# One run of weight loads behind layer 0's transposes, and 1/den of group 0 spread by PE

## The chip, the cores and the metric

The kernel runs on one core of a Trainium2 chip. The metric is the device time of one execution in microseconds (us). Every kernel was run several times beside the kernel before on the same chip; the medians and 95% intervals below come from those runs. Times inside an execution are counted from the first instruction of the profiled run of that kernel.

## The reference

Four layers over 2048 tokens of width 512, two of linear attention and two of a gated feed-forward block, in turn and with the same weights.

```python
def _A_ref(x, wqkv, wo):                         # 32 heads of 16
    q, k, v = ...                                # x @ wqkv, split into heads
    phi = lambda t: jnp.where(t > 0, t + 1, jnp.exp(t)) + 1e-6
    pq, pk = phi(q), phi(k)
    kv = jnp.einsum("bhsd,bhse->bhde", pk, v)
    z = jnp.einsum("bhsd->bhd", pk)
    num = jnp.einsum("bhqd,bhde->bhqe", pq, kv)
    den = jnp.einsum("bhqd,bhd->bhq", pq, z)[..., None] + 1e-6
    return merge_heads(num / den) @ wo
def _B_ref(x, w_gate, w_up, w_down):             # inner width 1792
    return (silu(x @ w_gate) * (x @ w_up)) @ w_down
x = A_x
for _ in range(2):
    x = x + _A_ref(_layernorm(x), A_wqkv, A_wo)
    x = x + _B_ref(_layernorm(x), B_w_gate, B_w_up, B_w_down)
```

## The kernel before

All five engines run hand-made orders. PE follows a list of tokens: `0k3` is layer 0, k of tile 3; `0q20` is q of group 2 (four tiles of 128 tokens), part 0; `0z` sums k over the tokens, `0d` makes den, `0r2` spreads 1/den of group 2 by PE, `0m` multiplies the k-v products by Wo, `0w` is the output matmul of the layer, `1u` gate and up, `1n` down, `S` a warming filler. The other engines have lists of the operations that belong to these tokens (`0x` is a layer norm, `xT` and `rT` are DMA transposes, `pqn` is the multiplication of q by 1/den). Each engine works strictly through its own list, so an operation that waits holds up all that stand behind it.

The weights but Wq, Wk and Wv are loaded by POOL, which has four DMA lanes; a DMA on a lane waits for the one before it on that lane.

```python
pr = Prog({"sp": 8, "act": 3, "pool": 4})        # DMA lanes of each issuing engine
...
weights = []
dma("sp", Wqkv[:, :, 0:D], wq3[:, :, 0:D], w=["Wq"])
dma("sp", Wqkv[:, :, 2 * D:], wq3[:, :, 2 * D:], w=["Wv"])
weights.append(lambda a: dma("pool", Wo[:], ..., w=["Wo"], after=a))
for c in range(NC):
    weights.append(lambda a, c=c: dma("pool", Wg[:, c, :], ...))
    weights.append(lambda a, c=c: dma("pool", Wu[:, c, :], ...))
def load_down(after): ...                        # Wd in four loads on POOL
...
last = list(xT_of.values())                      # layer 0's DMA transposes
for w_ in weights:
    w_(last)                                     # i.ld .. i.ld8 on POOL
```

Three steps on POOL make a mask of blocks of 16 by 16. Zm, the sum of k laid out for the den matmuls, needs that mask, and so every den matmul of layer 0 does.

```python
def z_fin(L, pb):
    op("dve", ..., r=[f"pb{pb}", "mask"], w=["Zm"], kind="zm")     # Zm = z * mask
```

POOL's order has the last mask step, `i.c7`, behind its nine loads: `... 0x14.negm i.ld i.ld1 ... i.ld8 i.c7 1x3.negm ...`.

A value of 1/den stands for 16 columns of q. There are two ways to spread it. Groups named in `PE_T` (group 2 here) go by PE: one DVE transpose, 16 matmuls with a selecting matrix into four PSUM banks, and four DVE multiplications from PSUM. The others go by DMA: for each tile ACT makes a repeated copy (`rrep`, a ring of three buffers), a DMA transposes it into RT, and DVE multiplies.

```python
for tl in range(TG):                             # by DMA
    q = r_rrep.take()
    op("act", ..., w=[f"rrep{q}"], kind="rep")
    op("sp", lambda e: e.dma_start(RT[R][:, :, ...], rrep[q][:], transpose=True), ..., kind="rT")
    scale(L, g, tl, RT[R][...], f"RT{R}_{tl}")   # kind "pqn" on DVE
def rep_pe(L, g):                                # by PE
    bs = [bank(pin=True) for _ in range(4)]
    for c in range(NC):
        for a, pb in enumerate(bs):
            mm(pb, esel[...], rT[d][...], n=P, ...)
    ...                                          # four multiplications on DVE read the banks
```

## Time and profile before

| | before |
|---|---|
| median of the first three runs (lowest to highest) | 430.45 us (429.04 to 430.57) |
| span of the profiled run | 428.1 us |
| first den, first Wo, first gate matmul of layer 1 | 42.56, 56.60, 68.80 us |
| first gate matmul of layer 3 | 276.48 us |

A fourth run, of 429.31 us, is counted in the result below and makes the median 429.88; the profiled run took 429.86. Two rows are added here that are needed later. The first, from the page, is the PE clock that was granted in 40 slices of the span, in tenths: full speed throughout. The second is from the view of the tile RT: how long the DMA transposes of 1/den take from issue to landing.

```profile
PEclk9999999999999999999999999999999999999999
```

```profile
DMA to landing us min/median/max: 2.4/2.4/4.5
```

### The profile page before, as it was taken

Reading aid. Unit: us, or ns where it says so; the run is one execution under the profiler, and the core shown is the slowest. Engines: PE = TensorE matmul, PEld = TensorE weight load, DVE = VectorE, ACT = ScalarE, POOL = GpSimd, SP = SyncE. Lnnn points to the kernel's source line nnn. Section 1 sums busy time; section 2 is a strip of 40 time slices with the busy share of each in tenths; the row PEclk is TensorE's granted clock in tenths of the full one; section 3 lists DMA queues with packets and bytes.
Section 4 is the critical chain, followed back from the end, with each engine's and each line's share of the span. In section 5 each row is a group of like instructions: output and inputs, shape, how many; then the busy total and the mean of one; then the engine's idle time right before and its main releaser. Section 6 shows DMA issues by size and latency. Waiting matters only on the chain.

```text
span 428.1 us, 6340 instructions
## 1 busy us (share of the span) xinstructions
PE 419.4 (98%) x2219; PEld 195.5 (46%) x2219; DVE 287.8 (67%) x629; ACT 202.9 (47%) x399; POOL 83.0 (19%) x205
## 2 busy tenths in 40 slices
PE   8999899999999999999999999999999999999997
PEld 6444444444444444444444444344444444444443
DVE  6865799793675476875447869888837606853662
ACT  5998785563356264254465648445312302402220
POOL 5634035210120150001334500431002000100000
PEclk9999999999999999999999999999999999999999
DMA  8639534522011021000021113322110010021001
GB/s 277 141 75 329 126 64 101 146 50 51 4 22 37 2 52 34 2 0 2 2 48 26 25 26 63 62 46 41 38 38 0 13 51 25 0 63 37 2 0 50
DMA packets 53279, 23.21 MB, mean 54 GB/s; under 512 B 46528, under 2 KB 52160, under 8 KB 53248
## 3 DMA queue, kind: packets, MB, share of 16 engines
q1 hardware_dynamic: 51408, 16.27, 17.6%
q0 software_dynamic: 1296, 6.03, 4.1%
q10 hardware_dynamic: 544, 0.52, 0.4%
q8 instruction: 17, 0.28, 0.3%
q14 instruction: 14, 0.11, 0.1%
HBM read 9.70 MB, written 2.10 MB: 28 GB/s over the span
## 4 chain that ended last, share of the span: by engine, by line
PE 88%; DMA 5%; ACT 3%; DVE 2%; issue 1%; SPq 0%; POOL 0%; ACTq 0%; DVEq 0%
PE pb L409 88%; DMA RT<-rrep 2%; DMA xnT<-xnA 1%; DMA X<-in_A_x_dram 1%; ACT pq L567 1%; ACT etmp L564 1%; ACT rrep L719 0%; DVE pq L573 0%; ACT GT L657 0%; DVE pq L732 0%; SPq L723 0%; ACT xnA L498 0%; SPq L440 0%; DVE xnA L522 0%; ACT xnA L495 0%
## 5 line engine op out<-in xcount | busy, mean ns | idle before, releaser
L782 ACT ACTIVATE tht<-pb 128x512 f32<-128x512 f32 x112 | 65.4, 595 | 129.4 <-PE pb L409 106.8
L409 PE MATMUL pb<-xnT,Wg 128*128 128x512 bf16 x448 | 115.0, 379 | 0.6 <-issue 0.6
L409 PE MATMUL pb<-xnT,Wu 128*128 128x512 bf16 x448 | 115.0, 379 | 0.0
L784 DVE SCALAR_TENSOR_TENSOR tht<-tht,pb 128x512 f32<-128x512 f32 x112 | 75.4, 684 | 55.6 <-ACT tht L782 48.9
L409 PE MATMUL pb<-Wd,hT 128*128 128x512 bf16 (+2 forms) x462 | 99.8, 373 | 0.0
L787 DVE TENSOR_TENSOR hT<-tht,pb 128x512 bf16<-128x512 f32 x112 | 74.2, 682 | 2.8
L409 PEld LDWEIGHTS pb<-Wd,hT 128*128 128x128 bf16 x462 | 44.7, 98 | 52.3 <-DVE hT L787 0.2
L409 PEld LDWEIGHTS pb<-xnT,Wu 128*128 128x128 bf16 x448 | 43.6, 98 | 53.1 <-DVE hT L787 0.8
L409 PEld LDWEIGHTS pb<-xnT,Wg 128*128 128x128 bf16 x448 | 43.5, 98 | 53.3 <-issue 1.3
L511 POOL TENSOR_TENSOR rstd<-vpe,negh 128x1 f32<-128x1 f32 x64 | 37.4, 587 | 90.4 <-DVE vpe L507 88.3
L564 ACT ACTIVATE etmp<-pb 128x512 bf16<-128x512 f32 x64 | 37.2, 594 | 21.8 <-PE pb L409 13.1
L501 POOL TENSOR_SCALAR mv<-sums 128x1 f32<-128x1 f32 x55 | 12.8, 239 | 119.8 <-DVE X L810 62.1
L409 PE MATMUL pb<-Wqkv,xnT 128*128 128x512 bf16 x128 | 31.2, 379 | 1.2 <-DMA xnT<-xnA 0.6
L409 PE MATMUL pb<-xnT,Wqkv 128*128 128x512 bf16 x128 | 32.1, 379 | 0.0
L409 PE MATMUL pb<-pk,xnA 128*128 128x512 bf16 x128 | 31.2, 379 | 0.0
L409 PE MATMUL pb<-GT,pq 128*128 128x512 bf16 x128 | 30.2, 379 | 0.2
L498 ACT ACTIVATE xnB<-X,sums 128x512 bf16<-128x512 bf16 x32 | 22.9, 717 | 15.7 <-DVE X L762 8.8
L569 DVE TENSOR_SCALAR etmp<-etmp 128x512 bf16<-128x512 bf16 x64 | 18.7, 304 | 12.1 <-ACT etmp L564 12.0
L762 DVE SCALAR_TENSOR_TENSOR X<-pb,X 128x512 bf16<-128x512 f32 x32 | 21.6, 686 | 7.1 <-PE pb L409 7.0
L810 DVE SCALAR_TENSOR_TENSOR X<-pb,X 128x512 bf16<-128x512 f32 x16 | 11.0, 689 | 19.1 <-PE pb L409 19.0
L498 ACT ACTIVATE xnA<-X,sums 128x512 bf16<-128x512 bf16 x23 | 16.5, 717 | 12.1 <-DVE X L810 11.9
L810 DVE SCALAR_TENSOR_TENSOR pq<-pb,X 128x512 bf16<-128x512 f32 (+2 forms) x17 | 10.9, 656 | 14.4 <-PE pb L409 14.3
(77 smaller groups left out, 309.9 us busy)
## 6 DMA issues: line engine op xcount, KB each, us to landing
out_dram<-pq SPq DMA_DIRECT2D x15, 128.0 KB, 1.8
Wg<-in_B_w_gate_dram POOLq DMA_DIRECT2D x4, 448.0 KB, 4.9
Wu<-in_B_w_up_dram POOLq DMA_DIRECT2D x4, 448.0 KB, 4.6
X<-in_A_x_dram SPq DMA_DIRECT2D x6, 256.0 KB, 4.8
Wd<-in_B_w_down_dram POOLq DMA_DIRECT2D x3, 512.0 KB, 4.7
Wqkv<-in_A_wqkv_dram SPq DMA_DIRECT2D x2, 512.0 KB, 7.0
Wqkv<-in_A_wqkv_dram ACTq DMA_DIRECT2D x2, 256.0 KB, 3.5
X<-in_A_x_dram SPq DMA_DIRECT2D x4, 128.0 KB, 3.4
```

The lines of the kernel that those rows point to most:

```text
L409: return op("pe", lambda e: e.matmul(o_ap, lhsT=lhsT, rhs=rhs, start=start, stop=stop, skip_group_check=skip), r=r, w=w, n=n)
L498: op("act", lambda a: a.activation(out=b_ap, in_=X[:, t, :], func=ACT.Square, scale=-float(D), bias=sums[:, t:t + 1], accum_out=mv[:, t, 1 ...
L501: op("pool", lambda p: p.tensor_scalar(out=mv[:, t, 0:1], in0=sums[:, t:t + 1], scalar1=-1.0 / D, scalar2=None, op0=ALU.mult), r=[f"sm{t}" ...
L511: op("pool", lambda p: p.tensor_tensor(out=rstd[:, t:t + 1], in0=vpe[:, t:t + 1], in1=negh[:], op=ALU.pow), r=[f"vp{t}", "negh"], w=[f"rs{ ...
L564: op("act", lambda a: a.activation(out=etmp[e][:], in_=PB[pb][:], func=ACT.Exp), r=[f"pb{pb}"], w=[f"e{e}"], kind="exp")
L567: op("act", lambda a: a.activation(out=dst, in_=PB[pb][:], func=ACT.Identity, bias=onep[:]), r=[f"pb{pb}", "onep"], w=dk, kind="id1")
L569: op("dve", lambda v: v.tensor_scalar(out=etmp[e][:], in0=etmp[e][:], scalar1=1.0, scalar2=1e-6, op0=ALU.min, op1=ALU.add), r=[f"e{e}"], w ...
L762: op("dve", lambda v: v.scalar_tensor_tensor(out=X[:, t, :], in0=PB[pb][:], scalar=1.0, in1=X[:, t, :], op0=ALU.mult, op1=ALU.add, accum_o ...
L782: op("act", lambda e: e.activation(out=tht[a][:], in_=PB[pg][:], func=ACT.Tanh, scale=0.5), r=[f"pb{pg}"], w=[f"th{a}"], kind="tanh")
L784: op("dve", lambda v: v.scalar_tensor_tensor(out=tht[a][:], in0=tht[a][:], scalar=1.0, in1=PB[pg][:], op0=ALU.add, op1=ALU.mult), r=[f"pb{ ...
L787: op("dve", lambda v: v.tensor_tensor(out=hT[h][:, j, :], in0=tht[a][:], in1=PB[pu][:], op=ALU.mult), r=[f"pb{pu}", f"th{a}"], w=[f"h{h}_{ ...
L810: op("dve", lambda v, pb=pb, lo=lo, hi=hi: v.scalar_tensor_tensor(out=o_ap[:, lo:hi], in0=PB[pb][:, 0:hi - lo], scalar=0.5, in1=X[:, t, lo ...
```

## The change

The intent, as far as the diff shows it, is to keep the weights away from the transposes: all that POOL loads, with Wv added, goes out in one run after layer 0's transposes and ahead of layer 1's, and group 0 of layer 0 needs no DMA transposes any more because PE spreads its 1/den. The core of the diff:

```diff
-dma("sp", Wqkv[:, :, 2 * D:], wq3[:, :, 2 * D:], w=["Wv"])
+weights.append(lambda a: dma("pool", Wqkv[:, :, 2 * D:], wq3[:, :, 2 * D:], w=["Wv"], after=a))
 ...
 for w_ in weights:
     w_(last)
+load_down(last)                        # was behind layer 1's first transposes
 ...
-    PE_T = 0d2 0t0 0t1 0t2 0t3 2d1 2z
+    PE_T = 0t0 0t1 0t2 0t3 2d1 0d0 0t14 0d2
-dsb, rtok, rT: 2 buffers;  rrep: 3
+dsb, rtok, rT: 3 buffers;  rrep: 2
 ... POOL's order:
-0x14.negm i.ld i.ld1 ... i.ld8 i.c7 1x3.negm ... Wd.ld3 ... Wd.ld1 Wd.ld2 ... Wd.ld ...
+0x13.pow i.ld i.ld1 ... i.ld9 Wd.ld Wd.ld1 Wd.ld2 Wd.ld3 i.c7 1x3.negm ...
 ... PE's order:
-0q31 0m0 0m1 0m2 0m3 0r2 0w3 ...
+0q31 0m0 0r0 0m1 0m2 0r2 0m3 0w3 ...
```

Two smaller things come with it: the transposes of tile 14 go by PE, and tile 12's k is summed on DVE instead of by PE (`0z12` becomes `0s`). The orders of ACT, DVE, POOL and SP are new throughout; among other things DVE takes over copies of PE's transposes from ACT.

## The prediction

> **What bounds the kernel now.** I read the page first (busy shares, chain), then PE's timeline for its idle time, then the timelines of POOL, DVE and ACT around each idle place.
>
> ```profile
> PE 419.4 (98%) x2219; PEld 195.5 (46%) x2219; DVE 287.8 (67%) x629; ACT 202.9 (47%) x399; POOL 83.0 (19%) x205
> ...
> PE 88%; DMA 5%; ACT 3%; DVE 2%; issue 1%; SPq 0%; POOL 0%; ACTq 0%; DVEq 0%
> ```
>
> PE works for 98% of 428.1 us and carries 88% of the chain of waits. The 98% alone would prove little, so I checked it by start times: in PE's timeline four 512-column matmuls start every 0.86 us.
>
> ```profile
> 1.24 4.44 PE L409 MATMUL pb<-hT 128*128 128x128 bf16 x42 [1.24 <-DVE hT L415]
> 7.07 1.02 PE L409 MATMUL pb<-Wqkv,xnT 128*128 128x512 bf16 x4 [0.51 <-DVE xnT L553]
> 15.69 1.90 PE L409 MATMUL pb<-Wqkv,xnT 128*128 128x512 bf16 x8 [0.58 <-DMA xnT<-xnA]
> ...
> 51.88 0.46 PE L409 MATMUL pb<-Zm,pq 128*128 128x8 bf16 x12 [1.33 <-DVE pq L573]
> ```
>
> These are all the PE rows of the first 230 us with idle time in front of them (42.56, quoted below, has only 0.22 us of lost start time). So what the change can win lies in two places: 0.58 us at 15.69 (PE waits for the first DMA transpose) and 1.33 us at 51.88. The other idle places (0.3 to 0.6 us each, 248 to 277 us) belong to layer 2. Every microsecond that PE is made to wait anywhere is, on the other hand, paid in full.
>
> The 1.33 us has this cause: DVE, which works in order, stands at the multiplication of q by the transposed 1/den of group 0 and waits for the DMA; the phi step that PE needs is behind it.
>
> ```profile
> 51.06 0.43 DVE L732 TENSOR_TENSOR pq<-pq,RT 128x512 bf16<-128x512 bf16 x1 [1.83 <-DMA RT<-rrep]
> 51.40 0.42 DVE L573 TENSOR_TENSOR pq<-pq,etmp 128x512 bf16<-128x512 bf16 x1
> ```
>
> Now POOL, whose 19% makes it look harmless, with the one DVE row that depends on it:
>
> ```profile
> 31.36 0.97 POOL L440 DMA_DIRECT2D Wo<-in_A_wo_dram  x1 [6.11 <-DMA xnT<-xnA]
> 32.33 0.57 POOL L440 DMA_DIRECT2D Wg<-in_B_w_gate_dram  x1
> 32.89 0.54 POOL L440 DMA_DIRECT2D Wu<-in_B_w_up_dram  x1
> 33.42 0.54 POOL L440 DMA_DIRECT2D Wg<-in_B_w_gate_dram  x1
> 36.58 0.56 POOL L440 DMA_DIRECT2D Wu<-in_B_w_up_dram  x1 [2.61 <-DMA Wo<-in_A_wo_dram]
> 37.70 0.65 POOL L440 DMA_DIRECT2D Wg<-in_B_w_gate_dram  x1 [0.56 <-DMA Wg<-in_B_w_gate_dram]
> 38.84 0.54 POOL L440 DMA_DIRECT2D Wu<-in_B_w_up_dram  x1 [0.49 <-DMA Wu<-in_B_w_up_dram]
> 39.96 0.54 POOL L440 DMA_DIRECT2D Wg<-in_B_w_gate_dram  x1 [0.59 <-DMA Wg<-in_B_w_gate_dram]
> 41.29 0.54 POOL L440 DMA_DIRECT2D Wu<-in_B_w_up_dram  x1 [0.79 <-DMA Wu<-in_B_w_up_dram]
> 41.83 0.37 POOL L430 TENSOR_SCALAR_AFFINE_SELECT mask<-mask 128x128 bf16<-128x128 bf16 x1
> ```
>
> ```profile
> 42.30 0.21 DVE L614 TENSOR_TENSOR Zm<-pb,mask 128x32 bf16<-128x32 f32 x1 [1.61 <-POOL mask L430]
> ```
>
> ```profile
> 42.56 0.56 PE L409 MATMUL pb<-Zm,pq 128*128 128x8 bf16 x16
> ```
>
> Four loads go out at once; from the fifth on POOL stands until the load four places earlier has landed (the program gives POOL four DMA lanes). Behind the ninth load stands the last step of the block mask. DVE waits 1.61 us for it to make Zm, and PE's first den matmul follows 0.26 us later. Before the change this costs PE only those 0.22 us: the queue of loads already ends exactly where PE begins to need the mask.
>
> **What the Trainium skill says.** (1) "Trainium Kernel Development and Optimization", Performance Expectations: matmul busy time is a bad measure of closeness to the roofline because matmuls are pipelined. The trace agrees: the page gives 379 ns for one matmul of 512 columns, while the starts are 0.86/4 = 0.215 us apart; hence I count starts. (2) "TensorE: Matmul & The Clock Gate", Part 1: the PE clock is halved by default and after about one idle window of 3.4 us, and takes about 3.4 us of work to return. The trace shows the cold half: the first 42 filler matmuls of 128 columns take 4.44 us, 106 ns each, the page's cold figure. No idle stretch of before is long enough to show the fall back; the change could make one. (3) "DMA: Bandwidth & Descriptors", SWDGE vs HWDGE vs iDMA: a DMA issued from GpSimd has its descriptors made in software on that engine. The trace agrees: each issue keeps POOL busy for 0.54 to 0.97 us, which the DMA queue of SP does not show as engine time. (4) The same page, Issuing engines are not separate DMA queues: all queues end on the same 16 engines, so moving Wv to POOL's queue moves its bytes in time but makes none of them cheaper.
>
> **The change part by part.**
>
> *Wv leaves the first run of loads on SP.* The trace has Wq landing at 12.14 and Wv at 13.74 us, the first transpose at 15.65. Without Wv that transpose could land up to 1.6 us sooner, and the 0.58 us at 15.69 may go. But the order on DVE puts the apply step of tile 4 behind three PE-transpose copies (0.41 us each, formerly on ACT) and a phi step (0.69), so its transpose is issued near 11.9 instead of 9.80 and I get it landing near 14.3. Walking PE's new order by 0.86 us a token, PE reaches the end of tile 5's k at about 18.0, where before had done the same work by 17.4. I book between -0.7 and +0.6 us. It does not matter, as the next point shows.
>
> *Wv, Wo, gate, up and Wd in one run.* The instruction order shows 14 loads in POOL's program (9 before), all in front of the last mask step, still four lanes, and the Zm instruction still waiting for POOL. The k-th load is issued when load k-4 has landed. In before: first load at 31.36, landed by 36.58 (5.2 us), then one per (41.29 - 36.58)/4 = 1.18 us for 448 KB. The 14th waits for the 10th: 5.2 + 9 x 1.18 + 0.2 (Wv is a second load of 512 KB) = 16.0 us after the first; its issue takes 0.8 (Wd in before: 0.75 to 0.84), the mask 0.4. The start: the last layer-0 transpose landed at 30.47 in before; now there are 11 instead of 12 (tile 14 goes by PE). Summing DVE's steps in the new order, tile 11's apply ends near 27.0 and its transpose lands near 29.4, so the loads start near 30.4. The mask is done at 30.4 + 16.0 + 0.8 + 0.4 = 47.6, Zm runs then, and PE's first den matmul starts at about 47.9 instead of 42.56: **5.3 us later**. PE should reach that place at 43.3 (42.3, plus 0.6 from the start, plus 0.25 for tile 14's four transposes, plus 0.1 for the four extra sum matmuls), so the trace should show some 4.5 us idle there.
>
> *Group 0's 1/den by PE.* It removes 4 ACT copies, 4 DMA transposes and 4 DVE multiplications of 0.43 us; it adds one DVE transpose (0.30), 16 matmuls on PE (0.6 us, as group 2's) and 4 DVE multiplications reading PSUM (0.68 us, 0.60 apart). The stall at 51.88 goes: 1.5 us by start times. But the first Wo matmul needs all four new multiplications: 2.5 us on DVE after the 16 matmuls, with only about 1.2 us of PE work between (three Wo-side matmuls, group 2's 16). That is about 1.3 us of new idle time just before Wo.
>
> *Sum.* From the first den matmul to the first Wo matmul before took 56.60 - 42.56 = 14.0 us, 11.85 of it work (1.5 stall and about 0.7 in small waits taken off). Now 47.9 + 11.85 + 0.6 + 1.3 = 61.65; walking DVE's backlog after the stall (one phi step more is left over) gives 62.2. I take 62.0: 5.4 us later than 56.60. From that token on PE's order is identical, and before had almost no idle time for 190 us, so nothing absorbs it: 430.45 + 5.4 = 435.85. If the clock falls during the 4.5 us, some 3.4 us at half speed cost 1.7; a window must lie wholly in the stall, about one in three: +0.6. Wd's loads no longer collide with layer 1's transposes (4.6 and 5.4 us against 2.4), but PE did not wait for those; with the 0.2 us wait near 98 us I take off 0.4. **436.0 us.**
>
> **Rivals.** *The gain as intended*: if POOL were not held (loads issued freely), PE would save 1.5 + 0.7 and pay 0.6 + 0.35 + 1.3, ending within 1 us of before, 429.5 to 431. Against it: the releases in POOL's rows. *The clock falls*: 437.5 to 438. *DVE becomes the bound after the stall*: it has 4 x 0.25 us more in this stretch and is 83% busy at 45 to 50 us; another 1 to 2 us, 437 to 438. *The stall is smaller*: if the loads stream faster or start at 29, 434.
>
> **Range and chances.** The mask's time is uncertain by about 1 us, the wait before Wo by 1, the clock by 1.7, layers 1 to 3 by 0.7: about 2.3 us together, a little wider above. Faster by 2% is impossible on a PE with 2 us to win. Slower by 2% is over 439.06.
>
> **What would show it.** Right: 14 loads on POOL, the last issued after 45 us; Zm waiting 4 to 6 us for the mask; PE idle 3 to 6 us before the first den matmul, at 46.5 to 49; no PE wait on RT near 52; about 1 us idle before the first Wo matmul, which starts at 60 to 64. The clock shows in the granted clock and in matmul starts 0.43 us apart just after the stall. Wrong: the mask done by 43, or PE meeting Wo before 58.

## The result, and the profile after

The changed kernel took **440.93 us** (median of four runs, 439.87 to 442.00), the kernel before 429.88 us beside it. The ratio is 1.0258, 95% interval 1.0224 to 1.0292: slower. A ratio here and below is the mean time of one kernel's fast runs over that of the other's of the same rounds, so it is not quite the ratio of the medians quoted.

The page of the changed kernel: PE is busy for about the same time (420.1 us, before 419.4) in a longer span, and the clock falls in the fifth slice.

```profile
PE 420.1 (96%) x2201; PEld 196.7 (45%) x2243; DVE 294.5 (67%) x636; ACT 199.6 (45%) x392; POOL 79.5 (18%) x205
...
PEclk9999699999999999999999999999999999999999
...
PE 79%; DMA 7%; DVE 7%; ACT 2%; issue 2%; POOL 1%; SPq 1%; DVEq 0%; POOLq 0%; ACTq 0%
```

PE's share of the chain of waits falls from 88% to 79%; DVE (2% to 7%) and DMA (5% to 7%) have most of what it lost. The timeline of POOL after (start, duration, then the idle time ahead and what ended it) shows why. There are 14 loads, of which three rows are enough, and the mask behind the last:

```profile
31.26 0.98 POOL L439 DMA_DIRECT2D Wqkv<-in_A_wqkv_dram  x1 [7.15 <-DMA xnT<-xnA]
...
41.32 0.54 POOL L439 DMA_DIRECT2D Wu<-in_B_w_up_dram  x1 [2.00 <-DMA Wu<-in_B_w_up_dram]
...
48.11 0.71 POOL L439 DMA_DIRECT2D Wd<-in_B_w_down_dram  x1 [0.41 <-DMA Wu<-in_B_w_up_dram]
48.83 0.37 POOL L429 TENSOR_SCALAR_AFFINE_SELECT mask<-mask 128x128 bf16<-128x128 bf16 x1
```

DVE's timeline has Zm waiting for it:

```profile
49.23 0.21 DVE L615 TENSOR_TENSOR Zm<-pb,mask 128x32 bf16<-128x32 f32 x1 [5.22 <-POOL mask L429]
```

These are all the rows of PE's timeline from 40 to 82 us with idle time ahead of them, and the one at 50.00, which has none but is slow:

```profile
49.58 0.56 PE L408 MATMUL pb<-Zm,pq 128*128 128x8 bf16 x16 [4.93 <-DVE Zm L615]
50.00 1.87 PE L408 MATMUL pb<-pk,xnA 128*128 128x512 bf16 x4
...
64.17 0.21 PE L408 MATMUL pb<-rT,esel 32*128 32x128 bf16 x1 [0.69 <-ACT pq L566]
65.06 0.40 PE L408 MATMUL pb<-rT,esel 32*128 32x128 bf16 x15 [0.67 <-ACT GT L657]
66.09 1.90 PE L408 MATMUL pb<-GT,pq 128*128 128x512 bf16 x8 [0.32 <-DVE pq L750]
79.38 0.81 PE L408 MATMUL pb<-xnT,Wg 128*128 128x512 bf16 x3 [0.92 <-DVE vpe L506]
```

The stall that the change was to take away (1.33 us at 51.88 before) is gone. In its place PE stands 4.93 us for the mask; the four matmuls at 50.00 start 0.427 us apart where 0.215 is normal; and there are three new waits before Wo and one before gate and up. The windows view gives busy times of PE, PEld, DVE, ACT and POOL, then the granted clock (1.00 is full), the DMA share and GB/s:

```profile
43.54:46.95 3.41, 1.03 (x13) 0.55 (x11) 0.47 (x2) 2.53 (x5) 2.05 (x3) 1.00 0.91 293
46.95:50.37 3.42, 0.79 (x17) 0.56 (x18) 1.11 (x5) 0.00 (x0) 1.82 (x3) 0.50 0.96 328
50.37:53.78 3.41, 3.41 (x13) 1.31 (x12) 1.66 (x5) 0.10 (x1) 0.00 (x0) 0.50 0.60 215
```

The clock is halved from 46.95 to 53.78 us. By stretches, the two profiled spans (428.09 and 439.03) differ so:

| stretch | before | after | difference | predicted |
|---|---|---|---|---|
| start to the first den matmul | 42.56 | 49.58 | +7.02 | +5.3 |
| den to the first Wo matmul | 14.04 | 16.51 | +2.47 | +0.1, and +0.6 for the clock |
| Wo to layer 1's first gate matmul | 12.20 | 13.29 | +1.09 | 0 |
| that to layer 3's first gate matmul | 207.68 | 208.21 | +0.53 | -0.4 to the end |
| the rest | 151.61 | 151.44 | -0.17 | |
| sum | 428.09 | 439.03 | +10.94 | +5.6 |

### The profile page after: what moved, and what is told of

Its sections match the earlier page's. It is cut to its first block, busy times and chain, and to the rows that moved or that the text cites. A ratio compares the mean times of both kernels' runs of the same rounds, so it can differ in the third digit from the quotient of the medians.

```text
span 439.0 us, 6322 instructions
## 1 busy us (share of the span) xinstructions
PE 420.1 (96%) x2201; PEld 196.7 (45%) x2243; DVE 294.5 (67%) x636; ACT 199.6 (45%) x392; POOL 79.5 (18%) x205
## 4 chain that ended last, share of the span: by engine, by line
PE 79%; DMA 7%; DVE 7%; ACT 2%; issue 2%; POOL 1%; SPq 1%; DVEq 0%; POOLq 0%; ACTq 0%
PE pb L408 79%; DMA Wu<-in_B_w_up_dram 2%; DMA xnT<-xnA 2%; DMA Wo<-in_A_wo_dram 1%; DMA X<-in_A_x_dram 1%; DVE pk L575 1%; ACT etmp L563 1%; DVE pq L750 1%; DVE etmp L568 1%; DMA xnT<-xnB 1%; DVE X L762 1%; SPq L439 1%; ACT xnB L497 1%; DVE xnA L521 1%; DVE GT L627 0%
## 5 line engine op out<-in xcount | busy, mean ns | idle before, releaser
L408 PE MATMUL pb<-xnT,Wg 128*128 128x512 bf16 x439 | 113.3, 379 | 1.5 <-DVE vpe L506 0.9
```

The source lines that it names most:

```text
L408: return op("pe", lambda e: e.matmul(o_ap, lhsT=lhsT, rhs=rhs, start=start, stop=stop, skip_group_check=skip), r=r, w=w, n=n)
```

## The experiments

Sixteen kernels ran, all with right results; they are told in the order of the argument. **Theory A** is the prediction's: the mask behind 14 loads makes PE stand, and the rest is small. Its rivals come up where they matter. In what was on record, letters of rivals are those of the respective runs.

### The mask's place in the changed kernel

`e1_mask_first` moves one POOL instruction of the changed kernel.

```diff
-... 0x15.pow 0x13.pow i.ld ... Wd.ld3 i.c7 1x3.negm ...
+... 0x15.pow 0x13.pow i.c7 i.ld ... Wd.ld3 1x3.negm ...
```

> The changed kernel with the last step of the block mask on POOL moved from behind the 14 loads to in front of them; nothing else. Theory A (the 4.93 us PE stands at the first den matmul are the wait for the mask behind the loads, and the 1.7 us of half-speed matmuls after it follow from that standstill): both go, 440.9 - 6.6 = 434.3 us, range 433.0 to 435.6; PE idle before the first den matmul under 0.5 us; granted clock 1.00 from 5 us on. Rival B (DVE and ACT were behind anyway, so PE would wait there for phi and PSUM banks): 438 to 441. What is left above before, about 4 us, would then belong to the new order of work, not to the mask.

Measured: 434.06 us, 1.0099 (1.0082 to 1.0116). The timeline of PE has this at the place of the 4.93:

```profile
44.17 0.54 PE L408 MATMUL pb<-Zm,pq 128*128 128x8 bf16 x16 [0.46 <-ACT etmp L563]
```

So the wait for the mask with all that follows from it is worth 440.93 - 434.06 = 6.9 us. But the changed kernel without this wait is still 1.0%, some 4 us, slower than before, which the prediction did not have.

### The two halves of the change alone

`e3_loads_only` gives the kernel before the one run of 14 loads and keeps everything else.

```diff
-dma("sp", ... w=["Wv"])                         # Wv joins POOL's run
+weights.append(lambda a: dma("pool", ... w=["Wv"], after=a))
+load_down(last)
-... i.ld8 i.c7 1x3.negm ... Wd.ld3 ... Wd.ld1 Wd.ld2 ... Wd.ld ...
+... i.ld8 i.ld9 Wd.ld Wd.ld1 Wd.ld2 Wd.ld3 i.c7 1x3.negm ...
```

> The kernel before with only the loads of the change: Wv and Wd join Wo, gate and up in one run of 14 on POOL behind layer 0's transposes, the mask step behind them as in before; order of PE, DVE and ACT as in before. Theory A: the mask is done 16.9 us after the first load (changed kernel: 31.26 to 48.11), near 48.3 to 49; PE comes to its first den matmul at 42.3 and stands 6 to 6.5 us, the clock falls (1.7), the old 1.5 us stall on the transposed 1/den may shrink or go since DVE catches up: 429.9 + 6.3 + 1.7 - 0 to 1.5 = 436.4 to 437.9, range 435.5 to 438.5. Rival C (the loads are harmless, the new order of work costs the time): 429 to 431.

Measured: 435.53 us, 1.0137 (1.0122 to 1.0152), with the granted clock at 0.992 in each run. In PE's timeline:

```profile
49.22 0.57 PE L409 MATMUL pb<-Zm,pq 128*128 128x8 bf16 x16 [7.21 <-DVE Zm L614]
```

PE came to this place earlier than in the changed kernel and stood longer, so the first den matmul starts at nearly the same time (49.22 and 49.58): the loads set it, not PE.

`e4_spread_only` gives the changed kernel the loads of before.

```diff
-weights.append(lambda a: dma("pool", ... w=["Wv"], after=a))
+dma("sp", ... w=["Wv"])
-... i.ld9 Wd.ld Wd.ld1 Wd.ld2 Wd.ld3 i.c7 ...
+... i.ld8 i.c7 ...                              # Wd's four loads among layer 1's norms
```

> The changed kernel with before's loads: Wv again on SP, Wd again behind layer 1's transposes, so 9 loads stand in front of the mask step; PE, DVE and ACT keep the changed order, with 1/den of group 0 spread by PE. Theory A: no wait for the mask (done near 42 to 43, PE comes at 44), no fall of the clock; what remains is the cost of the new order: about 434, range 432.5 to 435.5. Rival C' (the order is as good as before's, all of the loss is the loads): 429 to 431.5.

Measured: 435.59 us, 1.0129 (1.0108 to 1.0150), a little over what was expected. Three of its four runs had one halved window (clock 0.996) and took 435.6 to 435.9; the one with the full clock took 433.95. The two halves together make 1.37 + 1.29 = 2.66%, close to the 2.58% of the whole. The second half is thus as dear as the first. By stretches in its profiled run, against before: 2.3 us to the first den matmul, 0.4 from den to Wo, 2.1 from Wo to gate (with a halved window), 1.2 later. In the first of these PE waits 0.96 us at 18.04 for a transpose. It also waits 1.63 at 7.59 for DVE's copy of tile 0, but that copy is DVE's in both kernels: the same matmul started at 7.07 before, and between 7.08 and 7.60 in the other runs that keep the order of before, so this place differs from run to run and says nothing of the change.

### The loads against the transposes

`e5_loads_mask_first` is `e3_loads_only` with `i.c7` ahead of the loads. By theory A it should have been as fast as before.

> The kernel before with the one run of 14 loads, but the mask step in front of them. It tells the run of loads apart from the mask behind it (loads only, mask behind: 435.53). Theory A (the loads cost nothing but the late mask): the 7.4 us standstill and the fall of the clock go: 429.6 - 0.5 (Wv out of the way of the first transpose) = 429.1, range 428.3 to 430.3, granted clock 1.00. Rival D (the longer run of loads also slows the transposes of group 0's 1/den, issued at 45 to 49 us while loads land until 53): the old 1.5 us stall near 50 us grows to 3 or 4, 430.5 to 432.

Measured: **440.03 us**, 1.0240 (1.0218 to 1.0262). Theory A fell here: taking the wait for the mask away cost 4.5 us more than leaving it. PE's row, the row of DVE that held it, and the view of RT:

```profile
60.30 0.48 PE L409 MATMUL pb<-Zm,pq 128*128 128x8 bf16 x12 [10.50 <-DVE pq L573]
```

```profile
59.48 0.43 DVE L732 TENSOR_TENSOR pq<-pq,RT 128x512 bf16<-128x512 bf16 x1 [6.92 <-DMA RT<-rrep]
```

```profile
DMA to landing us min/median/max: 2.4/2.5/13.6
```

With the mask early, group 0's den is done while the run of loads is still under way, and its four transposes go out from 44.5 to 51.8 us among Wd's loads. They took 6.51, 13.64, 12.75 and 8.55 us, where the next ones, with no load in flight, took 2.4; Wd's loads took 5.65, 9.14, 11.95 and 11.78 us. In `e3_loads_only` the late mask held the same transposes back to 51.81 us and later; the last load landed at 53.21, and they took 2.4 to 4.4 us. Up to 4.5 us is no sign of loads: before, the transpose from 46.51 to 51.04 took that long though the last load had landed at 45.78.

`e8_wv_mask_first` tests this: as `e5_loads_mask_first`, but Wd's four loads stay where they were before.

```diff
-... i.ld9 Wd.ld Wd.ld1 Wd.ld2 Wd.ld3 1x3.negm ...
+... i.ld9 1x3.negm ... Wd.ld3 ... Wd.ld1 Wd.ld2 ... Wd.ld ...
```

> The kernel before with Wv moved behind the layer-0 transposes (10 loads on POOL), the mask step in front of the loads, and Wd's loads where they were, behind layer 1's transposes. Against the run of all 14 loads with the mask in front (440.03), where group 0's DMA transposes took 6.5 to 13.6 us beside loads that landed until 59.7. Theory E (the collision of Wd's loads with those transposes is what costs the 10 us): with Wd gone the loads end near 46.6, the transposes take 2.4 to 4.5 us as in the kernel before, and the start wins 0.5: 429.0, range 428.2 to 430.5. Rival F (any load beside the transposes is enough, or Wv's later landing holds KV): 433 or more.

Measured: **428.16 us**, 0.9959 (0.9945 to 0.9973). The views of RT and of PE:

```profile
DMA to landing us min/median/max: 2.4/2.5/4.3
```

```profile
51.12 0.46 PE L409 MATMUL pb<-Zm,pq 128*128 128x8 bf16 x12 [1.21 <-DVE pq L573]
```

The place of Wd's loads alone is worth 11.9 us once the mask is early. In `e8_wv_mask_first` three of the four transposes went out while gate and up loads were still landing (the last at 47.72) and took 3.5 to 4.3 us, so a few loads beside them are not enough. Whether it is the number of loads still to come or the kind of Wd's that makes 13.6 us was not tested.

The run with all 14 loads also shows what the spreading by PE is good for: with 14 loads and the mask in front, the kernel takes 440.03 us when group 0 goes by DMA and 434.06 us (`e1_mask_first`, though with its other orders too) when it goes by PE.

### The clock

The prediction gave the clock one chance in three. In the traces the halved stretches in the midst of a run last 3.41, 6.83 or 10.24 us; so a window, below, is a stretch of 3.41 us, laid so that a fall begins at its end. The changed kernel had 0.992, 0.992, 0.988 and 0.992 in its four runs: one window at half speed is 1.7 of some 439 us, 0.4%, so two windows in three runs and three in one.

The first tests filled the standstill with matmuls of zeros, 128 columns each, as in the warm-up. `e2_filler` has 64 of them in a bank of their own, `e7_filler_same_banks` puts the 64 into the bank of group 0's den, which leaves the rotation of the banks alone, and `e12_filler_full` has 92 there.

```diff
-... 0q13 0s 0d02 ...
+... 0q13 0s F F F ... F 0d02 ...
+if tok == "F":
+    mm(fb, zero[:, 0:P], zero[:, 0:P], True, True, ..., n=P, cols=(0, P))
+    continue
```

> The changed kernel with 64 filler matmuls of 128 columns on zeros put on PE just before its first den matmul, inside the stall (64 x 0.056 = 3.6 us of the 4.9). The mask is as late as before. Theory A: the fall of the clock is a cost of its own, 1.7 us: 440.9 - 1.7 = 439.2, range 438.5 to 440.0, granted clock 1.00 throughout, matmul starts 0.216 us apart after the stall. Rival B (the half-speed matmuls hide behind DVE's backlog): 440.5 to 441.5 although the clock stays up.

> The filler run again, mended: the first one took a PSUM bank of its own and so moved every later bank by one, and its wait before group 2's spreading matmuls grew from 0.85 to 1.87 us. Now the 64 fillers write the den bank of group 0 before its first den matmul, and all other banks stay as in the changed kernel. Theory A: the clock does not fall at the mask, 440.9 - 1.7 = 439.2, range 438.2 to 440.2, granted clock 0.996 to 1.00 against 0.988 to 0.992. Rival B (half-speed matmuls hide behind other engines): 440.5 or more with the clock up.

> As the second filler run, with 92 instead of 64 fillers, 5.1 us, the whole standstill of the changed kernel. The 64 left 1.6 us idle and the clock still fell for one window of 3.4 us (51.7 to 55.1), so they did not test what they were made for. Theory A (half-speed matmuls after the standstill cost 1.7 us of time): no half-rate window between 45 and 56 us, 440.9 - 1.7 = 439.2, range 438.2 to 440.3; a window may still fall at the waits before the first Wo matmul in some runs. Rival B (they hide behind DVE and ACT): 440.5 or more with the clock up.

Measured: 443.26, 440.13 and 440.03 us; 1.0313 (1.0285 to 1.0341), 1.0248 (1.0216 to 1.0280), 1.0230 (1.0205 to 1.0255). `e2_filler` is a miss: the extra bank shifted the rotation, and the wait before group 2's spreading grew from 0.85 to 1.87 us. In `e7_filler_same_banks` 1.6 us stayed idle and the clock still fell, from 51.65. `e12_filler_full` fills the standstill, and its windows show the full clock at the place in question:

```profile
46.00:50.00 4.00, 4.00 (x70) 3.41 (x68) 1.86 (x8) 0.00 (x0) 1.32 (x3) 1.00 0.95 300
50.00:54.00 4.00, 4.00 (x38) 2.10 (x37) 3.39 (x9) 1.32 (x3) 0.00 (x0) 1.00 0.38 130
```

Its stretch from den to Wo took 14.97 us (48.49 to 63.46) instead of 16.51: **1.54 us is what the clock cost there**. The median gained only 0.9: three of its four runs had one halved window (0.996, 439.3 to 441.4, against 438.36 with the full clock, which is the profiled one). Where in those three it fell is not on record.

The second tests make PE stand for chosen times in a kernel that is otherwise undisturbed: `e8_wv_mask_first` with the last mask step behind the ten loads, done once, four times or ten times (0.37 us each; the result is the same).

```diff
-... 0x14.negm i.c7 i.ld ... i.ld9 1x3.negm ...
+... 0x14.negm i.ld ... i.ld9 i.c7 [i.c8 i.c9 i.c10 [... i.c16]] 1x3.negm ...
```

> e8 with the mask's last step behind the tenth load instead of ahead of the first: PE should stand about 2.2 us before the first den matmul (mask near 43.2, PE ready at 41.6), and the wait of 1.2 us near 51 should shrink, because the transposes of group 0 then go out later. Theory W (the clock falls only after a window of 3.41 us without work): clock 1.000 in all runs, 429.0 to 429.8. Theory H (a window in which PE is busy for some 1.9 us or less is enough): in some runs a halved window (clock 0.996), each of these 1.5 to 1.7 us longer.

> As e15_stall_0 with the mask's last step done four times (0.37 us each, the result is the same): PE stands about 3.3 us, less than one window. Theory W: clock 1.000 in all runs, 430.0 to 430.9. Theory H: 3.3 us of idle time leave at least one window with no more than 1.8 us of work whatever the phase, so the clock falls in every run (0.996 or less), 431.6 to 432.6.

> As e15_stall_0 with the mask's last step done ten times: PE stands about 5.5 us. Theory W: a whole idle window in about 60% of the runs, so runs of 432.2 to 433.0 and of 433.9 to 434.7 beside each other. Theory H: every run at 0.992 or 0.996, 433.8 to 436.

| | PE stood | runs (granted clock) | median, ratio |
|---|---|---|---|
| e15_stall_0 | 1.55 us | 429.28 to 430.29 (1.000 in all) | 429.84, 1.0003 (0.9988 to 1.0018) |
| e15_stall_3 | 3.19 us | 431.52, 432.01, 432.46 (0.996), 433.44 (0.992) | 432.24, 1.0062 (1.0043 to 1.0082) |
| e15_stall_9 | 6.00 us | 433.68 to 434.42 (0.992 in all) | 433.80, 1.0099 (1.0082 to 1.0116) |

A standstill of 3.19 us, which is shorter than a window, brought the clock below full in all four runs, while 1.55 us did so in none; where it fell is known for the profiled run. (The wait near 51 us, which `e15_stall_0` was to shrink, stayed at 1.21.) The windows view of `e15_stall_3` shows that the window ahead of the fall was not idle:

```profile
40.87:44.28 3.41, 0.81 (x3) 0.19 (x2) 0.00 (x0) 2.96 (x5) 2.20 (x6) 1.00 0.98 341
44.28:47.70 3.42, 2.75 (x22) 1.32 (x23) 2.50 (x8) 0.81 (x2) 0.21 (x1) 0.50 0.51 205
47.70:51.11 3.41, 3.41 (x13) 1.29 (x12) 1.57 (x4) 1.70 (x4) 0.00 (x0) 0.50 0.38 77
```

Theory W, that a whole window must be idle, is refuted; theory H, that a mostly idle one is enough, holds for what was asked. Where exactly the limit lies stays open. `e1_mask_first`, with no wait over 0.7 us in this part, has a fall behind a window half full of small matmuls with short waits between them (in its profiled run; the other three kept the full clock):

```profile
56.31:59.72 3.41, 1.73 (x21) 0.82 (x22) 3.10 (x7) 3.05 (x6) 0.00 (x0) 1.00 0.19 38
59.72:63.13 3.41, 3.41 (x10) 1.18 (x8) 2.88 (x7) 0.81 (x2) 1.44 (x5) 0.50 0.19 38
```

In the changed kernel the windows from 60.61 to 64.02 (2.82 us busy) and 64.02 to 67.43 (2.27) were followed by none. But the busy time alone does not sort all windows: one with 2.35 us in `e10_r0_alone` was followed by a fall, one with 1.48 us in `e16_rrep2` (the one from 47.97 to 51.38) was not. The windows of `e1_mask_first` and `e10_r0_alone` hold the spreading's matmuls, which use 32 of the 128 rows; whether such work counts for less was not tested.

### Spreading group 0 by PE, alone

`e10_r0_alone` takes the kernel before, mask step ahead of the loads, and sends only group 0 by PE; the four evacuations of `0m` go to ACT. A third den buffer did not fit beside three `rrep` buffers, so `rrep` has two, as in the changed kernel. `e11_r0_early` has `0r0` two tokens of q sooner.

```diff
-PE_T: 0d2 ...        dsb, rtok, rT: 2   rrep: 3
+PE_T: 0d0 0d2 ...    dsb, rtok, rT: 3   rrep: 2
-0v 0q31 0m0 0m1 0m2 0m3 0r2
+0v 0q31 0m0 0r0 0m1 0m2 0r2 0m3                 # e10
+0v 0r0 0q31 0m0 0m1 0m2 0m3 0r2                 # e11
```

> The kernel before with 1/den of group 0 spread by PE and nothing else of the change (loads as before; the mask step in front of them; all four M copies on ACT, as the change has them). Theory A: the 1.5 us stall on the transposed 1/den goes (and 0.2 at the mask), 16 matmuls come in (0.6), and the first Wo matmul waits 1.3 to 2.3 us for the four new multiplications on DVE: 429.6 - 1.7 + 0.6 + 1.3 to 2.3 = 429.8 to 430.8; 1.5 more where that wait makes the clock fall. Rival (the spreading is a gain by itself, as intended): 427.5 to 428.6.

> As the run with group 0's spreading alone, but its 16 matmuls stand one q projection earlier on PE (before 0q31 instead of behind the first M matmul), so DVE's four multiplications start some 0.9 us sooner relative to the first Wo matmul. Theory A (the wait in front of Wo is set by when those multiplications can start): 0.5 to 1.2 us less than that run, and the idle time before the first Wo matmul down to about 0.5 to 1 us. Rival (the wait is for banks and the M copies on ACT): no difference.

Measured: 432.89 us, 1.0086 (1.0066 to 1.0106), and 433.38 us, 1.0100 (1.0075 to 1.0125). Both miss: the first lies 2 us above theory A's range, the second did not gain. From den to Wo `e10_r0_alone` took 14.68 us (42.29 to 56.97), 0.6 more than before: the old stall of 1.33 is gone, and the 16 matmuls (0.6 us) and four waits of 0.23 to 0.33 us around group 2's spreading and Wo came. An earlier start did not help, so it is not the start of the multiplications that PE waits for; group 2's matmuls wait for banks, which DVE's multiplications free one by one some 0.75 us apart. The larger part of the loss lies in layer 2: from layer 1's first gate matmul to layer 3's it took 210.05 us instead of 207.68.

`e16_rrep2` asks whether that is the smaller ring: before, mask step first, two `rrep` buffers, nothing else by PE.

```diff
-rrep = [sb("rrep", ...) for _ in range(3)]
+rrep = [sb("rrep", ...) for _ in range(2)]
```

> The kernel before with the mask's last step ahead of the loads and two buffers instead of three for the repeated 1/den, nothing by PE but what was. If the smaller ring is what e10 and e11 lose in layer 2: the waits near 263 (here some 261), 272 and 279 are back, layer 1's first gate matmul to layer 3's takes some 210 us instead of 207.7, and the time is 431 to 432. If the ring is innocent: 429.3 to 430.0 as the kernel before, and the loss belongs to the group that goes by PE.

Measured: 440.24 us, 1.0244 (1.0214 to 1.0274), far more than either theory had. The part that was asked is answered: the same stretch took 287.05 - 75.89 = 211.16 us, and the waits of layer 2 are back. PE's timeline, first of `e10_r0_alone`, then of `e16_rrep2`:

```profile
263.04 0.40 PE L409 MATMUL pb<-rT,esel 32*128 32x128 bf16 x16 [1.09 <-DVE rT L714]
```

```profile
49.90 0.24 PE L409 MATMUL pb<-Zm,pq 128*128 128x8 bf16 x4 [2.27 <-DVE pq L576]
56.05 0.48 PE L409 MATMUL pb<-Zm,pq 128*128 128x8 bf16 x12 [3.30 <-DVE pq L573]
...
268.23 0.41 PE L409 MATMUL pb<-rT,esel 32*128 32x128 bf16 x16 [1.17 <-DVE rT L714]
```

What was not foreseen is layer 0: ACT's second copy, at 47.59, stood 2.56 us until the first transpose had landed, PE waits 2.27 and 3.30 us, and the clock falls as well (54.80 to 61.62). It was the second copy and not the third because buffers are given out in the program's order (tiles 0, 1, 2, 3), while ACT's list keeps the order of before (`0d0.rep 0d0.rep2 0d0.rep1 0d0.rep3`): with two buffers, tiles 0 and 2 share one. Group 3's list was fitted to two buffers in this run and in `e10_r0_alone`, group 0's was not. So the 440.24 us is the price of two buffers with this list; how much of it a mended list would save was not tested. The changed kernel, with its own order of layer 2 for two buffers, lost only 0.53 us on that stretch (0.9 in `e7_filler_same_banks` and 1.8 in `e12_filler_full`).

### A version from what was learned

`e9_order_fixed` is `e8_wv_mask_first` with two swaps, so that the phi step that PE needs stands ahead of the multiplication that waits for RT.

```diff
 DVE:
-0d0.pqn2 0q23.phi 0G1.evac
+0q23.phi 0G1.evac 0d0.pqn2
 ACT:
-0d1.rep1 0G0.evac 0G2.evac 0G3.evac
+0G0.evac 0G2.evac 0G3.evac 0d1.rep1
```

> The run with Wv moved and the mask first, with two swaps of order: on DVE the phi step of 0q23 and the copy of G1 go in front of the first multiplication that waits for a transposed 1/den; on ACT the three G copies go in front of the copy for group 1 that waits for a free buffer. Both are what held PE for 1.5 us near 50 us in the kernel before. Expected if that stall is only an order on DVE and ACT: 1.3 us less than the run without the swaps, 427.7, range 426.8 to 429.0, no PE idle time near 50 us. If the stall only moves on to the next wait for the same transposes (the first Wo matmul): no difference.

Measured: **427.89 us**, 0.9949 (0.9936 to 0.9961). It beats both kernels, and `e8_wv_mask_first` by only 0.3 us, which these runs do not make certain; 1.3 had been expected. PE's timeline shows where it went:

```profile
50.45 0.46 PE L409 MATMUL pb<-Zm,pq 128*128 128x8 bf16 x12 [0.75 <-DVE pq L573]
53.86 1.02 PE L409 MATMUL pb<-Wo,KVT 128*128 128x512 bf16 x4 [0.32 <-DVE KVT L669]
55.57 2.07 PE L409 MATMUL pb<-GT,pq 128*128 128x512 bf16 x8 [0.34 <-DVE GT L660]
```

The wait near 51 fell from 1.21 to 0.75, and the multiplications that now come later push DVE's KVT and GT back, for which PE waits 0.32 and 0.34 us. The wait moved on instead of going away.

`e14_order_fixed_wv_sp` is the same with Wv back on SP.

> The kernel before with the mask first and the two swaps of order, Wv still in the first loads on SP: does Wv's move pay? Expected 429.6 - 0.2 - 1.3 = 428.1, range 427.2 to 429.2; 0.4 to 0.6 more than with Wv moved if the first transpose's wait behind Wv (0.75 us) is what Wv costs; less than with Wv moved if the longer run of loads disturbs group 0's transposes.

Measured: 429.14 us, 0.9980 (0.9968 to 0.9993). Wv's move is worth 1.2 us, more than the 0.4 to 0.6 expected: it is the part of the change that pays.

## Why the prediction was wrong

**The direction and the main mechanism were right.** POOL's 14 loads hold the mask step, Zm waits 5.22 us for it and PE 4.93, and moving this one step takes 6.9 us away (`e1_mask_first`). The stall on RT went as said, and the DMA transposes of 1/den that remain all took 2.4 to 2.5 us. The result lay 4.9 us above the prediction, where 2.3 us of uncertainty had been booked. Four terms of its sum were mis-sized; a fifth did not count here but did in the experiments.

**The mask's time: 47.9 predicted for the first den matmul, 49.58 measured, 1.7 us.** The loads began at 31.26, not 30.4, because the last layer-0 transpose landed at 30.52 instead of 29.4: DVE came to tile 11 later than the sum of its steps said. And the fourteenth load went out 16.85 us after the first, not 16.0: the fourth load, Wu, took 7.47 us to land, so POOL stood 2.00 us at 41.32, a hole that a rate of 1.18 us per load does not have. The same hole, of 1.5 to 2.0 us, appears in all six profiled runs with the changed orders, `e4_spread_only` with its nine loads among them (in `e2_filler` and `e12_filler_full` one load later). With the orders of before, no run waits over 1.0 us at the eighth or ninth load. So the hole goes with the new orders; why was not tested. It is not the whole error either: `e3_loads_only` has no hole and still needed 16.87 us, so the rate itself was set too fast.

**The clock: "a window must lie wholly in the stall, about one in three: +0.6".** The step failed by its rule, not by bad luck. A mostly idle window is enough; the one before the fall held 1.03 us of work, and a standstill of 4.93 us leaves such a window whatever the phase. `e15_stall_3` shows it with 3.19 us in four runs of four. The cost, 1.54 us, was near the 1.7 of the text, but no run was free of it: all four ran below the full clock. (The rival's 437.5 to 438 does not follow from the sum either: 436.0 less the 0.6 booked, plus 1.7, is 437.1.)

**From den to Wo: 14.1 predicted, 16.51 measured.** Of the 2.4 us over it the clock is 1.54. The rest, some 0.9, is a chain of waits: 1.3 us were booked for new idle time just before Wo, but PE lost time at three places, 64.17, 65.06 and 66.09 (0.85, 0.88 and 0.49 us by start times, 2.2 together). They follow on banks that ACT's steps and DVE's four multiplications (3.06 us together, where 2.5 had been booked) give back one after the other. `e11_r0_early` shows that starting them sooner does not help.

**"From that token on PE's order is identical, ... so nothing absorbs it", and 0.4 us taken off.** Nothing absorbed it, but something was added: 1.09 us from Wo to gate, with 0.92 us of waiting at 79.38 for a layer norm on DVE, and 0.36 later. I had compared PE's order and not what the new DVE order does there. The 0.92 is not a fixed price, however: with the same orders `e7_filler_same_banks` and `e12_filler_full` took 12.34 and 12.28 us from Wo to gate, without that wait, and lost 0.9 and 1.8 us in the stretch after it. No experiment took this part alone; that the new orders lose 1 to 2 us after Wo is read from the traces, and the cause stays open.

**The fifth term is the price of the spread with its new orders.** The prediction put the new start of layer 0 at -0.7 to +0.6 us and added that it did not matter. In the changed kernel this is so, because the loads set the time of the first den matmul. But PE reached that place at 44.5, not at 43.3 as said, and once the mask is early the price shows: `e1_mask_first` is 1.0% and `e4_spread_only` 1.3% slower than before. So the rival "the gain as intended", given as within 1 us of before if POOL were not held, was wrong too: the nearest to it that ran, `e1_mask_first`, takes 434.06 us. The 2.3 us in the start of layer 0 of `e4_spread_only` are read from its trace and not taken apart.

**What the prediction did not see at all** is the collision of loads and transposes, because the late mask hid it. Its only word on collisions was that PE did not wait for those of layer 1. `e5_loads_mask_first` against `e8_wv_mask_first` puts 11.9 us on it. Keeping many loads and transposes apart thus matters. But the collision that costs so much is made by the long run itself: with Wd behind layer 1's first transposes, where it was before, group 0 could stay with DMA at 428.16 us.

## What to carry to other kernels

A long run of loads on an engine with few lanes makes that engine's whole order wait for landings, so a small computation that another engine needs, such as the mask, belongs ahead of it. Two effects can hide each other: test a part of a change together with its partner and alone, since a late mask kept transposes out of the loads' way, and removing it made the kernel 4.5 us slower in one combination and 6.9 us faster in another. When PE is the bound, count a wait of some 3 us with the half-speed time that follows it: 1.54 us in the changed kernel, and some 2.6 in the profiled run of `e15_stall_3`, where two windows fell (den to Wo took 15.28 us, against 13.92 in `e15_stall_0` of which 1.21 was another wait).

## What the Trainium skill lacked or had wrong

- "TensorE: Matmul & The Clock Gate", Part 1, has the clock fall after at least one idle window of about 3.4 us. Here windows in which PE was busy 0.81 us (`e15_stall_3`, a gap of 3.19 us) and 1.73 us (`e1_mask_first`, no wait over 0.7 us there) of 3.41 were followed by halved ones. The page's section "A second HAM failure mode: psum-queue depth-cycling" says that micro-idles between groups of matmuls can do it, which agrees, but gives no share of busy time; the runs put it near half a window, not sharply (a fall after 2.35 us, none after 1.48).
- The same page, Part 1, has the clock return after a busy window, which agrees, but again with no share: a halved window with 2.75 us of work was followed by another halved one (`e15_stall_3`), one with 2.89 us by the full clock (`e16_rrep2`, 58.21 to 61.62).
- "DMA: Bandwidth & Descriptors", Rules for kernel authors, says that a transpose next to ordinary DMAs needs nothing. The row is about the data, and the results were right in all runs. What the page lacks is a word on the time: it has all DMAs end on the same 16 engines, as the prediction cites, but gives no figure for a transpose among loads. Transposes of 2.4 us took 6.5 to 13.6 us beside Wd's loads, and a load up to 11.95 us (`e5_loads_mask_first`).
